# A condition product over 128 rows, a gate-bias product moved, and a new order for an adaLN transformer block

## The chip, the core and the metric

The kernel runs on one NeuronCore of a Trainium2 chip. It is one launch. The metric is the device time of that launch in microseconds; lower is better. The core has five engines with a queue each: TensorE (PE, matmuls and transposes), VectorE (DVE), ScalarE (ACT), GpSimd (POOL) and SyncE (SP, which here issues DMAs). Each engine executes its queue in order and waits on semaphores for the others.

## The reference

A block of a transformer with a condition vector c. Two halves, each behind a layer norm that the condition scales and shifts; the first half is attention over 8 keys at distances 0, 2, ... 14, the second an MLP.

```python
x = A_x                                               # 1 x 2048 x 448, bf16
mod = (silu(c) @ w_mod).reshape(1, 6, 1, 448)         # c is 1 x 448
sa, ca, ga, sb, cb, gb = mod[:, 0], ..., mod[:, 5]
h = layernorm(x) * (1 + ca) + sa
x = x + ga * A_ref(h, A_wqkv, A_wo)                   # 16 heads of 28, window 8, dilation 2
h = layernorm(x) * (1 + cb) + sb
x = x + gb * B_ref(h, B_w1, B_b1, B_w2, B_b2)         # layernorm, 448 -> 1792, tanh-Gelu, 1792 -> 448
```

In B_ref the last step is `h @ w2 + b2`, so the output holds `gb * b2`, the gate-bias product.

## The kernel before

**Tiles.** Even and odd positions are kept apart (`NS = 2`), since the dilation is 2. The 2048 positions are 8 tiles p = 0 to 7 of 2 x 128 positions (`NP = 8`). Attention works on 9 batches of 114 positions of each parity (`NB = 9`), the MLP on 4 pairs of tiles t (`NT = 4`). PSUM is cut into four slots of two banks (room "P"); every PSUM tile lives in one of them.

**A written-out order.** The kernel is a list of tasks (`Plan.add`), each with an engine, a function that issues its instructions, what it reads and writes, and the buffers it uses. `Plan.emit` then issues the tasks in the order of the string `ORDER`; a buffer's slot comes from the list `SLOTS`. So the order of each engine's queue is the order of that engine's tasks in `ORDER`. An entry is a task's number in order of creation; `79:A` puts the task on ScalarE (D: VectorE, P: GpSimd), `88:R` takes TensorE's variant with the half-height rest first, and `52+9@52` first issues 9 filler matmuls of zeros (128x128 by 256 columns, function `filler`, L369) into the PSUM tile of task 52. A task added to the list shifts the numbers of all later ones.

**The head.** `c_cols` (L374) turns the row c into columns: matmuls of c_row, one partition high, with a row of ones, for 4 pieces of 112, each issued twice. From it come `e_c`, `silu`, `silu_bc` (c's silu, broadcast), then `mod_cols` (L390, 40 matmuls: shift and scale of the first norm as columns) and `sca`, which the evacuation of the first transposes needs (`evac_h`, L471: hT = transposed norm x scale + shift). Meanwhile x of tile 0 goes through `stats`, `rstd`, `norm`, `tail` and `tr0` (transposes on TensorE, L506). Tiles 0 to 3 are transposed on TensorE, tiles 4 to 7 by DMA (zT). The q and k weights come from HBM packed (wqk_st for the first 384 rows, wqr_st for the last 64) and are spread to 32 columns a head by `spread` and `spread r` (L412); `qk0_0af0`, ... `qk0_1b` are the q (0) and k (1) products of tile 0 (`f0` to `f2`: the three full contractions; `r`: the half-height rest).

**mods** (L592) computes the other four condition rows (ga, sb, 1 + cb, gb), writes them to HBM (`mod_st`) and loads them back broadcast over the partitions (`mod_bc`, L607). Then VectorE scales wo by ga (`wo_scale`, L610) and w2 by gb (`w2_scale`, L618), and GpSimd makes `gbb2 = gb * b2` (L614). `residual` (L796) adds gbb2 to x for each tile (x1p, GpSimd), and `fin` (L847) adds that to the MLP's output. A one-column copy on GpSimd, `gate` (L826), waits for the first Gelu of an MLP pair, so that the x1p of that pair start no earlier.

**The stages** (loop over `PHASES`): batches 0 to 4 of attention and MLP pair 0; batches 5, 6 and pair 1; batches 7, 8 and pairs 2, 3. Names in what follows: `lt` are the logits of a batch, `pd` its denominators, `po` its outputs (128 matmul and weight-load instructions a batch), `v` its values, `omul` the normalised output, `wo0` to `wo7` the output projections with `x1` (the residual add), `w1_t_g` and `w2_p_n_k` the MLP's products.

Of the kernel before, what the change touches and what calls it, by code (L numbers as in the profile page):

```python
# [9 lines left out]
FP32 = mybir.dt.float32  # L10
BF16 = mybir.dt.bfloat16
# [6 lines left out]
KM, MW = 4, 112  # L18
# [31 lines left out]
]  # L50
ORDER = """
0 13 3 15 1 4 5 14 11 7 16 12 17 8 18 9 10 19 6 52+9@52 2 20 60 21 58 22 61 53 59 54 23 62 55 56 63 57 64 65 24 66
67+13@68 25 68 26 76 70 69 27 77 71 73 72 28 78 74 75 84+10@84 29 85 96 79:A 86 30 82:A 98 31 80:A 97 81 83:A 87+1@90
88:R 32 99 130 100 120 101 90 91 89 92 33 103 93 102 94:R 34 118 104:A 35 121 105 131 119 128 95 36 164 106 129 109:A
179 107:A 37 189 166 108:A 180 122 169 132 190 165 123 187 209 244 38 167 133 188 256 170 110 191 245 168 39 135 210
111:R 171 134 113 40 124 125 112:D 192 114:R 126:A 41 136 127 177 115 137 42 194 150 178 193 139:A 43 138 195 211 44
181 140 151 182 141 212 196 214 172 246 173 215 183 247 147 257 184 174 248 254 185 152 249 45 255 175 258 186 146:R
213 149 251 250 176 259 252:A 143 46 260 253 261 216 262:A 276 145 148:D 153 263 217 277:D 218 219 142 197 200:A 199
198 47 220 48 205:R 49 144 221 50 51 418:A 278 154 281 201 279 155 267 156 207 266 264 159 206:R 282 280 203 160 316
283 265:A 222 162 208 163 527 317 272 161 223 157 284 285 274:D 286 202 287 224 226 269:R 225 288 204 227 158 289 271  # L60
228 318 229 351 290 419 352 230 231 291 273:R 420 293 292 454:A 232 348 294 353 275 313 311 233 295 349 236 296 234
314 268 237 297 298 312 315 299 319 270 346 350 235 300 321 238 301 239 116 320 347 303 354 302 240 322 355 304 117
241 455 305 242:D 356 306 323 243 357 307 528:R 308 456:D 309:A 381 310 324 358 529 563 359 325 326 387 360 328 363
329 327 364 361 382:R 330 389 362 331 365 390 366 391 388 333 368 332 367 397 384 334 383 369 335 385 392:R 370 399
338 400 402 398 336 386 339 404 373 337 371 403 424 374 340 372 395 413 375 393 376 396 401 394 411 417 377 378 341
412 425 343 460 342 379:A 426 421 380 344:A 457 461 414 458 345 462 405 422 415 459 416 406 423 427 428 429 464 407
430 431 564 463 565:D 408 465 506 466 409 490 467 410 491:R 508 507 468 492 493 509 511 494 432 469 495 513 470 496
510 433 512 471 472 434 473 436 501:R 474 435 437 499 475 438 497 439 498 500 477 440 441 476 514 442 502 478 505 443
503 516 479 504 446 526 480 517 444 481 447 445 530 482 566 448 531 533 483 449 515 484 534 532 520 567 451 535 450
568 569 518 485 536 570 521 452 538 519 486 453 571 537 487 539 573 572 522 488:A 540 574 489 575 541 599 576 523 542  # L70
577 524 543 525 600 578 544 545 581 546 579 547 582 615:R 580 548 604 583 603 584 601 605 550 617 586 585 616 549 587
602 551 588 610:R 552 606 591 618 620 609 553 607 555 622 608 554 589 619 556 592 590 557 631 593 611 594 613 612 558
623 614 596 559 560 632 595 561:D 621 562 629 597 598 630 624 633 625 634 626 635 627 628 640:R 636 637 653 656 639
638 657 655 645 644 641 654 643 642 650:R 648 647 646 664 651 652 658 649 665 659 666 667 660 672 661 668 662 673 669
663 674 675 670 671
# [76 lines left out]
def kernel(  # L152
# [65 lines left out]
    c_row = cst.tile([1, D], BF16, name="c_row")  # L218
    one1 = cst.tile([1, 128], BF16, name="one1")
# [21 lines left out]
    one = add("DVE", 0.06, lambda: nc.vector.memset(one1[:], 1.0), writes=["one1"], after=[zero], name="one1")  # L241
# [89 lines left out]
    add("ACT", 0.4, lambda: nc.scalar.dma_start(out=c_row[:], in_=c), writes=["c"], late=1.8, name="load c")  # L331
    tbl0 = add("ACT", 1.28, lambda: nc.scalar.preload_act_table_set(EXP_SET), name="tbl")
    load_x(0, 1)
    KP = (range(KM - 1), range(KM - 1, KM))
# [578 lines left out]
```

## Time and profile before

| | |
|---|---|
| three runs | 175.27, 175.70, 180.20 us; median 175.7 us |
| the profiled execution | 175.99 us, of which the span from the first to the last instruction is 174.3 us |
| TensorE, VectorE, ScalarE, GpSimd busy | 166.9, 117.6, 103.9, 42.0 us |
| instructions on TensorE | 2152 matmuls, 2152 weight loads |
| DMA | 15.12 MB, nearly all of the input in the first 45 us |

The table reads so: TensorE has something in flight for nearly the whole span, and the other engines have room on average, but not in each stage. Durations in the profile's rows overlap where an engine is pipelined; the distance between the starts of two rows is what a group costs in the stream.

### The profile page before, as it was taken

What the parts mean: (1) busy time and instruction counts of PE and PEld (TensorE: products, weight loads), DVE (VectorE), ACT (ScalarE), POOL (GpSimd) and SP (SyncE); (2) the same over time, 40 slices, a digit from 0 to 9 for tenths busy, and PEclk for the clock granted to TensorE, in tenths of its full rate; (3) what the DMA queues carried; (4) which work ended last, traced back from release to release, by engine and by line L of the source; (5) the groups of instructions that cost most, each with busy time, mean ns of one, the idle gap of its engine ahead of it and who ended that gap; (6) DMA issues with size and microseconds to landing.
All of it is one profiled execution on the core that took longest, in us unless ns stands there. A gap on an engine that the chain in (4) does not pass through costs nothing.

```text
span 174.3 us, 4984 instructions
## 1 busy us (share of the span) xinstructions
PE 166.9 (96%) x2152; PEld 85.4 (49%) x2152; DVE 117.6 (67%) x290; ACT 103.9 (60%) x146; POOL 42.0 (24%) x60
## 2 busy tenths in 40 slices
PE   7999989999999999999999999997999999999993
PEld 5876564444434355335564343464444455444562
DVE  6498999869989999897436368966498852200103
ACT  3279688699548994587944926769408730078300
POOL 6000624020020120377000183040007940071000
PEclk9999999999999999999999999999999999999999
DMA  5999979996000033000350100008410018200002
GB/s 162 322 323 314 237 217 249 230 259 203 4 2 4 0 66 60 4 0 0 40 141 4 53 0 0 0 4 86 95 53 2 0 26 113 92 0 0 0 30 79
DMA packets 20708, 15.12 MB, mean 87 GB/s; under 512 B 13705, under 2 KB 19726, under 8 KB 20686
## 3 DMA queue, kind: packets, MB, share of 16 engines
q1 hardware_dynamic: 20684, 14.80, 35.6%
q8 instruction: 17, 0.28, 0.7%
q14 instruction: 5, 0.04, 0.1%
q10 hardware_dynamic: 2, 0.00, 0.0%
HBM read 9.81 MB, written 1.84 MB: 67 GB/s over the span
## 4 chain that ended last, share of the span: by engine, by line
PE 72%; DMA 11%; DVE 10%; issue 2%; SPq 2%; ACT 1%; DVEq 0%
PE p L841 25%; PE p L527 21%; DMA x_all<-in_A_x_dram 8%; PE pw L761 6%; PE p L533 4%; PE pq L527 4%; DMA mod_bc<-mod_hbm 3%; PE pv L527 3%; PE lt L696 2%; PE po L729 2%; PE pv L664 2%; DVE w_s L618 2%; DVE et L709 1%; DVE hT L476 1%; DVE stt L432 1%
## 5 line engine op out<-in xcount | busy, mean ns | idle before, releaser
L822 ACT ACTIVATE hm<-p,b_col 128x512 bf16<-128x512 f32 x56 | 33.9, 690 | 33.4 <-PE p L533 30.8
L841 PE MATMUL p<-w_s,hm 128*128 128x448 bf16 (+1 forms) x238 | 44.4, 342 | 1.6 <-issue 1.6
L527 PE MATMUL p<-yT,w_s 128*128 128x512 bf16 x168 | 38.5, 380 | 0.0
L841 PEld LDWEIGHTS <-hm 128*128 128x128 bf16 x238 | 22.7, 98 | 20.8 <-issue 2.4
L448 POOL TENSOR_TENSOR rs_all<-tv_all,neg_half 128x2 f32<-128x2 f32 x22 | 16.2, 745 | 66.4 <-DVE tv_all L446 50.3
L847 DVE TENSOR_TENSOR x_all<-p,x1p 128x896 bf16<-128x896 f32 (+2 forms) x10 | 9.0, 903 | 25.7 <-PE p L841 25.7
L527 PEld LDWEIGHTS <-w_s 128*128 128x128 bf16 x168 | 15.8, 98 | 21.1 <-issue 3.4
L527 PE MATMUL pq<-hT,Wqk 128*128 128x512 bf16 (+1 forms) x108 | 22.2, 345 | 0.4 <-DVE x_all L768 0.4
L432 DVE BATCH_NORM_STATS2 stt<-x_all 128x6 f32<-128x448 bf16 x32 | 18.7, 609 | 1.2 <-DMA x_all<-in_A_x_dram 1.2
L703 ACT ACTIVATE et<-lt 128x928 bf16<-128x928 f32 x18 | 16.3, 954 | 4.0 <-PE lt L696 4.0
L799 POOL TENSOR_TENSOR x1p<-x_all,gbb_bc 128x448 f32<-128x448 bf16 x16 | 16.2, 1040 | 0.0
L527 PEld LDWEIGHTS <-Wqk 128*128 128x128 bf16 x108 | 9.4, 97 | 10.3 <-issue 3.7
L746 DVE TENSOR_TENSOR qT<-po,den 128x912 bf16<-128x912 f32 x9 | 9.9, 1100 | 6.2 <-ACT den L740 6.2
L709 DVE TENSOR_TENSOR et<-et,mask 128x928 bf16<-128x928 bf16 x18 | 11.3, 633 | 3.6 <-ACT et L703 3.6
L761 PE MATMUL pw<-wo_s,qT 128*128 128x448 bf16 x64 | 13.1, 353 | 0.4 <-DVE qT L746 0.4
L768 DVE TENSOR_TENSOR x_all<-pw,x_all 128x896 bf16<-128x896 f32 x8 | 8.7, 1083 | 6.6 <-PE pw L761 6.6
L738 ACT ACTIVATE den<-pd 128x928 f32<-128x928 f32 x9 | 8.5, 944 | 6.9 <-PE pd L718 6.9
L826 POOL COPY seen<-hm 128x1 bf16<-128x1 bf16 x4 | 3.9, 980 | 31.3 <-ACT hm L822 31.3
L740 ACT ACTIVATE den<-den,den_bias 128x928 f32<-128x928 f32 x9 | 9.6, 1067 | 0.2
L761 PEld LDWEIGHTS <-qT 128*128 128x128 bf16 x64 | 6.1, 98 | 6.5 <-DVE qT L746 0.9
L432 DVE BATCH_NORM_STATS2 stt<-h 128x6 f32<-128x448 bf16 x16 | 9.2, 609 | 0.0
L777 DVE TENSOR_TENSOR h<-h,mod_bc 128x896 bf16<-128x896 bf16 x16 | 9.1, 614 | 0.0
(101 smaller groups left out, 191.1 us busy)
## 6 DMA issues: line engine op xcount, KB each, us to landing
wmod<-in_w_mod_dram SPq DMA_DIRECT2D x4, 392.0 KB, 11.3
w_s<-in_B_w_dram SPq DMA_DIRECT2D x7, 224.0 KB, 4.6
out_dram<-x_all SPq DMA_DIRECT2D x7, 224.0 KB, 2.0
x_all<-in_A_x_dram SPq DMA_DIRECT2D x3, 448.0 KB, 5.4
w_s<-in_B_w_dram SPq DMA_DIRECT2D x3, 448.0 KB, 4.2
wqk_st<-in_A_wqkv_dram SPq DMA_DIRECT2D x3, 225.0 KB
wm_st<-in_w_mod_dram SPq DMA_DIRECT2D x1, 588.0 KB, 4.8
x_all<-in_A_x_dram SPq DMA_DIRECT2D x2, 224.0 KB, 2.6
```

The lines of the kernel that those rows point to most:

```text
L432: add("DVE", 0.53, lambda: nc.vector.bn_stats(out=stt[:, w, b, :], in_=src()), reads=reads, bufs=bufs, after=early if w == b == 0 else (), ...
L448: add("POOL", 0.55 + 0.17 * n, lambda: nc.gpsimd.tensor_tensor(out=r, in0=tv, in1=neg_half[:, 0:n], op=ALU.pow), reads=[f"tv{w}_{b0}", "ne ...
L527: nc.tensor.matmul(out(), lhsT=lhs(kt, slice(0, 128)), rhs=rhs(kt, slice(0, 128)), start=first and kt == 0, stop=not first and kt == KT - 2)
L703: exps.append(add("ACT", 0.83, lambda half=half, lt=lt: nc.scalar.activation(out=et.t[:, 2 * half:2 * half + 2].rearrange("p r m c -> p r ...
L709: nc.vector.tensor_tensor(out=ev, in0=ev, in1=mask[:], op=ALU.mult)
L740: exps.append(add("ACT", 0.96, lambda: nc.scalar.activation(out=den.t[:], in_=den.t[:], func=ACT.Exp, scale=-1.0, bias=den_bias[:]), bufs= ...
L746: nc.vector.tensor_tensor(out=qT[:, :, LEAD + q00:LEAD + q00 + 2 * WQ], in0=po.t[:, :, 0:NS * 4 * WQ].rearrange("p j (m c) -> p m j c", c=WQ),
L761: nc.tensor.matmul(pw.t[:, s, 0:D], lhsT=qT[:, NS * PLACE[ft] + s, LEAD + 128 * p:LEAD + 128 * p + 128], rhs=wo_s[:, ft, :], start=(ft == ...
L777: add("DVE", 0.55, lambda vec=vec, op=op: nc.vector.tensor_tensor(out=h2.t[:], in0=h2.t[:], in1=vec.unsqueeze(1).to_broadcast([128, NS, D] ...
L799: add("POOL", 1.0, lambda n=n: nc.gpsimd.tensor_tensor(out=x1p.t[:, n, :], in0=xn(p, n), in1=gbb2_bc[:], op=ALU.add), reads=[f"x{p}", "gbb ...
L822: gelus.append(add("ACT", 0.585, lambda f=f, a=a, p1=p1s[g]: nc.scalar.activation(out=hm.t[:, f].rearrange("p n c -> p (n c)"), in_=p1.t[: ...
L841: nc.tensor.matmul(p2.t[:, n, 0:c1 - c0], lhsT=hm.t[:, f, n, q * 128:(q + 1) * 128], rhs=w2_s[:, f, c0:c1], start=(f == parts[0][0]), stop ...
```

## The change

Four edits. **c_row** becomes 128 partitions high; VectorE fills it with zeros first (new task `c0`, number 1), the DMA writes c into its first row, `one1` is 128 rows of ones, and `c_cols` contracts over 128 rows, once for each of the 4 pieces instead of twice. **gbb2** is created in `mlp` for pair 0, behind `gate`, instead of in `mods`. The **zero matmuls** go from 33 (9 before c_cols, 13 before mod_cols, 10 and 1 in qk0) to 25 (11, 10, 4). **ORDER and SLOTS** are new lists.

```diff
-    c_row = cst.tile([1, D], BF16, name="c_row")
-    one1 = cst.tile([1, 128], BF16, name="one1")
+    c_row = cst.tile([128, D], BF16, name="c_row")
+    one1 = cst.tile([128, 128], BF16, name="one1")
...
-    one = add("DVE", 0.06, lambda: nc.vector.memset(one1[:], 1.0), writes=["one1"], after=[zero], name="one1")
+    zero_c = add("DVE", 0.17, lambda: nc.vector.memset(c_row[:].bitcast(FP32), 0.0), writes=["c"], after=[zero], name="c0")
+    one = add("DVE", 0.1, lambda: nc.vector.memset(one1[:], 1.0), writes=["one1"], after=[zero_c], name="one1")
...
-    add("ACT", 0.4, lambda: nc.scalar.dma_start(out=c_row[:], in_=c), writes=["c"], late=1.8, name="load c")
+    add("ACT", 0.4, lambda: nc.scalar.dma_start(out=c_row[0:1, :], in_=c), writes=["c"], late=1.8, name="load c")
...
-        for k in [*range(KM)] * 2:
-            nc.tensor.matmul(psc.t[0:MW, 0, 128 * k:128 * k + 128], lhsT=c_row[0:1, k * MW:(k + 1) * MW], rhs=one1[:], start=True, stop=True)
-
-    add("PE", 0.9, c_cols, mode="32x128", reads=["c", "one1", "warm_w"], bufs=[psc], fills=[psc], name="c_cols")
+        for k in range(KM):
+            nc.tensor.matmul(psc.t[0:MW, 0, 128 * k:128 * k + 128], lhsT=c_row[:, k * MW:(k + 1) * MW], rhs=one1[:], start=True, stop=True)
+
+    add("PE", 0.45, c_cols, mode="F", instr=8, reads=["c", "one1", "warm_w"], bufs=[psc], fills=[psc], name="c_cols")
...
-        add("POOL", 1.05, lambda: nc.gpsimd.tensor_tensor(out=gbb2_bc[:], in0=gb_bc, in1=b2_bc[:], op=ALU.mult),
-            reads=["gb", "b2"], writes=["gbb2"], port=True, name="gbb2")
...
+        if t == 0:
+            add("POOL", 1.05, lambda: nc.gpsimd.tensor_tensor(out=gbb2_bc[:], in0=gb_bc, in1=b2_bc[:], op=ALU.mult),
+                reads=["gb", "b2"], writes=["gbb2"], port=True, after=[gate], name="gbb2")
```

The two lists, read out by the tasks' names, where the queues differ most (`#` counts the tasks of one name in order of creation; in `stats` and `norm`, #5 and #6 belong to tile 2, #7 and #8 to tile 3, #9 to #12 to tiles 4 and 5, #17 and #18 to tile 6, #19 and #20 to tile 7):

```
ScalarE, head
 before: load c, table load, e_c, ln, rstd, silu_bc, evac_h#1, evac_h#3, spread r x4, ln#2, rstd#2, evac_qk#1, ...
 after:  table load, load c, ln, e_c, rstd, silu_bc, spread#4, evac_h#1, spread r#2, evac_h#3, spread r#1, ln#2, ...
VectorE, from tile 2's stats on
 before: ... evac_h#5, aggr#7, stats#10, stats#12, aggr#10, tv#1, tv#2, aggr#12, stats#11, stats#17, aggr#11, stats#20,
         tv#4, aggr#17, mask#1, norm#8, mask#2, norm#7, norm#5, norm#6, ...
 after:  ... stats#10, aggr#5, evac_h#8, tv#1, stats#19, stats#17, aggr#19, stats#12, aggr#17, aggr#10, stats#20,
         norm#8, norm#7, aggr#20, norm#5, stats#11, mask#2, aggr#11, tv#8, norm#6, ...
SP, behind the w1 loads
 before: zT5, mod_st, w2l0, zT4, w2l1, zT6, mod_bc, zT7, w2l2, w2l3, w2l4, w2l5, w2l6
 after:  w2l0, w2l1, mod_st, w2l2, w2l3, zT4, zT5, zT7, mod_bc, zT6, w2l4, w2l5, w2l6
TensorE, qk0
 before: qk0_0af0, 0af1, 0af2, (1 zero), 0ar, 0b, 1af0, 1af1, 1af2, 1ar, 1b
 after:  qk0_0af0, 0af1, 1af0, 1af1, 0af2, 0ar, 0b, 1af2, 1ar, 1b
TensorE, from mods to wo0
 before: lt1 x2, pd0, po0, qk2_1b, qk2_1a, qk2_0b, v2, pd1, po1, qk2_0a, qk4_1a, lt2 x2, qk4_0a, qk4_1b, lt3_1, wo0
 after:  lt1 x2, b1, qk2_0b, qk2_0a, qk2_1a, pd1, qk2_1b, pd0, po1, v3, lt2 x2, v2, po0, qk4_1b, v5, po2, pd2, wo0
TensorE, batches 7 and 8
 before: ..., lt8_1, pd7, w2_3_0_1, po7, po8, pd8, w2_3_1_0, wo6, w2_3_1_1, wo7, w1_2_0, ...
 after:  ..., lt8_1, w2_2_0_1, w2_3_0_0, po7, pd7, w2_3_1_0, w2_3_1_1, po8, pd8, w2_3_0_1, wo6, w1_2_0, w1_2_6, wo7, ...
```

Twenty-eight other tasks change their engine, mostly evacuations that either ScalarE or VectorE can do. `spread#4`, the k half of the weight spread (128x1536), goes from VectorE to ScalarE.

More of the change, by code (lines that the diff above doesn't have):

```diff
@@ L57 @@
[L57 to L61, printed above, removed]
@@ new lines @@
+101 87 131 88 102 89:R 34 103 132 104 35 93 130 121 94 90 36 95:R 133 105:D 122 134 119 37 106 96 179 164 120 110 38
+107:A 123 254 124 109:A 244 169 108:A 166 255 189 39 165 209 245 180 256 167 136 40 135 170 114 257 125 187 137 210
+115:R 171 41 188 177 111 116 258 126 190 259 178 112:R 42 246 127:A 181 191 43 247 182 128 248 113 138 44 261 151
+142:A 45 139 249 141 211 46 152 192 140 214 47 212 117 144 153 251 215 193 213 48 183 216 143:R 184 49 194 185:D 250
+168 147 252:A 118 195 146:D 186 217 260 148 149:D 219 196 262:A 145:D 220 172 218 150 311 263 221 174 278 175 312:D
@@ L76 @@
+646:R 637 640 654 658 639 638 657 656 665 647 648 655 650 673 649 669 674 661 675 676 662 659 660 666 663 670 667 664
+671 668 672
 """
```

36 lines of the change are left out of this document (17 added, 19 removed), and 10 rows, old and new, of the table SLOTS.

## The prediction

> **What bounds the kernel now.** I read the page first: busy times, then the chain that ended last.
>
> ```profile
> span 174.3 us, 4984 instructions
> ...
> PE 166.9 (96%) x2152; PEld 85.4 (49%) x2152; DVE 117.6 (67%) x290; ACT 103.9 (60%) x146; POOL 42.0 (24%) x60
> ...
> PE 72%; DMA 11%; DVE 10%; issue 2%; SPq 2%; ACT 1%; DVEq 0%
> ```
>
> TensorE is busy 96% of the span, and 72% of the chain is TensorE. So an edit is worth what it takes out of TensorE's stream, or out of the waits in that stream. Next I listed those waits, in the timeline of TensorE.
>
> ```profile
> 22.06 1.06 PE L509 MATMUL ptr<-ident,zy 128*128 128x128 bf16 x16
> ...
> 24.18 0.37 PE L598 MATMUL pb<-wmod,silu_bc 112*32 112x448 bf16 x4 [0.31 <-DMA wmod<-in_w_mod_dram]
> ...
> 25.30 0.44 PE L696 MATMUL lt<-qT,kT 28*64 28x58 bf16 x32 [0.38 <-DVE hT L476]
> ...
> 26.55 1.47 PE L527 MATMUL pq<-hT,Wqk 128*128 128x512 bf16 x6
> ...
> 31.50 1.64 PE L664 MATMUL pv<-Wv,hT 128*64 128x448 bf16 x16
> ...
> 46.23 1.45 PE L527 MATMUL pq<-hT,Wqk 128*128 128x512 bf16 x6 [0.42 <-DVE x_all L768]
> ...
> 50.03 1.69 PE L761 MATMUL pw<-wo_s,qT 128*128 128x448 bf16 x8 [0.41 <-DVE qT L746]
> ```
>
> ```profile
> 122.43 1.49 PE L841 MATMUL p<-w_s,hm 128*128 128x448 bf16 x7 [1.57 <-issue]
> ```
>
> Five waits, 0.31 + 0.38 + 0.42 + 0.41 + 1.57 = 3.09 us, are nearly all there is after the first 14 us. The last and largest is ended by "issue": TensorE waited for no engine and no tile. The changed kernel issues the same matmuls after that point, and counting from the two orders, its stream changes array shape as often (83 times in both), so nothing is won or lost there. What can change is the head, and these waits.
>
> **The head: c_cols, the zeros, the queues.** The old head:
>
> ```profile
> 0.80 0.50 ACTq L331 DMA_DIRECT2D c_row<-in_c_dram  x1
> ...
> 1.33 1.28 ACT L332 ACT_TABLE_LOAD   x1 [1.33 <-PEq L897]
> ...
> 1.59 0.81 DVE L301 MEMSET wo_s<- 128x896 f32 x1 [0.23 <-issue]
> ...
> 3.16 1.10 PE L377 MATMUL ps_c<-one,c_row 1*112 1x128 bf16 x8
> 3.39 1.16 DVE L432 BATCH_NORM_STATS2 stt<-x_all 128x6 f32<-128x448 bf16 x2 [0.32 <-DMA x_all<-in_A_x_dram]
> ...
> 6.93 1.06 PE L509 MATMUL ptr<-ident,zy 128*128 128x128 bf16 x8
> ...
> 7.31 0.29 DVE L419 COPY Wqk<-wqk_st 128x512 bf16<-128x512 bf16 x1 [1.01 <-DMA wqk_st<-in_A_wqkv_dram]
> ...
> 9.43 1.02 ACT L478 ACTIVATE hT<-ptr,mod_col 128x256 bf16<-128x256 bf16 x2 [3.80 <-DVE mod_col L409]
> ...
> 10.34 1.43 ACT L428 COPY Wqr<-wqr_st 64x256 bf16<-64x256 bf16 x4
> ...
> 11.52 0.39 PE L533 MATMUL pq<-hT,Wqr 64*128 64x256 bf16 x3 [0.17 <-ACT Wqr L428]
> ...
> 12.71 1.01 ACT L587 CAST qT<-pq 128x1024 bf16<-128x1024 f32 x1
> ```
>
> ```profile
> L369 PE MATMUL ps_col<-warm_w x13: 393/421/421, 4.2 to 6.7; 128*128 128x256 bf16 x13
> L369 PE MATMUL pq<-warm_w x11: 272/273/283, 9.1 to 10.9; 128*128 128x256 bf16 x11
> ```
>
> The zero-fill of c_row is a new VectorE memset of 224 fp32 per partition; by wo_s (896 in 0.81) it is about 0.2 us, and VectorE has 0.32 idle before the first x arrives: nothing. The c load now waits for it and stands behind the table load: issued at about 2.1 instead of 0.8. Eleven zero matmuls at the old spacing (nine from 1.12 to about 3.04, 0.213 each) end at 3.5, so c is about in time, and four full-height matmuls replace eight one-row ones (about 0.55 less). The old head has TensorE at half speed until some time between 6.7 and 9.1 (421 ns, then 273 ns for the same matmul). If full-height c_cols let it speed up earlier, the first transposes (8 in 1.06 at 6.93) shrink by about half a microsecond.
>
> But the new ScalarE queue puts the k half of the weight spread (`spread#4`, 128x1536) ahead of the first hT evacuation. It needs all three wqk loads: the first is in at 7.3, the other two at about 8.5 (an estimate: 450 KB at 0.37 MB per us, the mean of this window).
>
> ```profile
> 7.30:8.00 0.70, 0.70 (x14) 0.70 (x12) 0.29 (x1) 0.00 (x0) 0.00 (x0) 1.00 1.06 385
> 8.00:8.60 0.60, 0.60 (x30) 0.56 (x26) 0.00 (x0) 0.00 (x0) 0.00 (x0) 1.00 1.10 351
> ```
>
> ScalarE takes 0.36 for 256 columns and 1.01 for 1024, so about 1.45 for 1536: until 10.0. Then hT (0.51), one Wqr copy (0.36), hT (0.51), one Wqr copy (0.36): Wqr is complete at about 11.75, where the old one let TensorE go at 11.52. From there the old stream took 2.73 us to the end of qk0 at 14.25; the new one has two k pieces (0.44) behind it already: 14.05. The head gives at most 0.2, and the next paragraph takes that away.
>
> **x for tiles 6 and 7.** In the chain and in VectorE's timeline:
>
> ```profile
> 9.47 8.77 DMA x_all<-in_A_x_dram
> ```
>
> ```profile
> 15.99 1.15 DVE L432 BATCH_NORM_STATS2 stt<-x_all 128x6 f32<-128x448 bf16 x2 [0.53 <-DMA x_all<-in_A_x_dram]
> ...
> 18.26 0.63 DVE L432 BATCH_NORM_STATS2 stt<-x_all 128x6 f32<-128x448 bf16 x1 [0.32 <-DMA x_all<-in_A_x_dram]
> ...
> 19.55 0.61 DVE L709 TENSOR_TENSOR et<-et,mask 128x928 bf16<-128x928 bf16 x1
> ...
> 20.93 1.00 DVE L452 TENSOR_SCALAR zy<-x_all,mvs,rs_all 128x448 bf16<-128x448 bf16 x3
> ```
>
> The loads' order on SP is unchanged, so x[6:8] still lands at 18.24. The old VectorE came to its first use at 17.9; the new queue has it (`stats#19`) earlier, right after one hT evacuation and `tv#1`. After x[4:6] at 15.97 stand one stats (0.53), an aggr, an hT and tv, so VectorE is there at about 17.0 and waits 1.2. Behind it stand the norms of tiles 2 and 3, for which TensorE's tr2 waits: five stats at 0.53, four norms at 0.31, one mask at 0.54, small ones 0.5: 4.9 us, done at 23.2 against 21.9. TensorE wants tr2 at 22.06: a new wait of 1.1. The waits of 0.31 and 0.38 behind it (w_mod in at 24.15; hT) are then covered by it, but hT of tiles 2 and 3 comes about 0.9 later too. I take +0.6 net; from -0.3 (x earlier, old waits gone) to +1.4.
>
> **gbb2.** GpSimd's product now waits for the first Gelu:
>
> ```profile
> 38.08 2.00 DVE L610 TENSOR_TENSOR wo_s<-wo_s,mod_bc 128x896 bf16<-128x896 bf16 x2 [0.81 <-DMA mod_bc<-mod_hbm]
> ...
> 40.98 0.61 DVE L618 TENSOR_TENSOR w_s<-w_s,mod_bc 128x896 bf16<-128x896 bf16 x1
> ```
>
> ```profile
> 38.14 1.46 POOL L614 TENSOR_TENSOR gbb_bc<-mod_bc,b_bc 128x448 f32<-128x448 bf16 x1 [8.95 <-DMA mod_bc<-mod_hbm]
> ```
>
> Beside it the two wo_scale took 2.00, where two of that shape take at most 1.22 (the w2_scale of 0.61): 0.78 goes away, just where VectorE feeds TensorE's waits of 0.42 and 0.41. I take these two in full, -0.83, bounds 0 and -0.83. Behind the first gate the product delays four x1p and two rstd by 1.5; their users, the final adds and the norms of tiles 2 and 3, wait for TensorE in between, so I put nothing on it. Nor on the end, where the same stores leave in another order.
>
> **The wait at 120.9.** Just before it TensorE ran its two densest groups back to back, and one instruction packet was in flight:
>
> ```profile
> 118.97 1.36 PE L729 MATMUL po<-et,vb 64*32 64x57 bf16 x128
> ```
>
> ```profile
> q8 instruction: 17, 0.28, 0.7%
> ```
>
> ```profile
> q8 instruction: 1, 0.02, 5.7%
> ```
>
> Seventeen packets carry 4304 TensorE instructions, so 256 each; the one in the stretch 119.2 to 121.3 took 5.7% of 16 engines over 2.1 us, that is 1.9 us of one. The two po are 256 instructions in 1.3 us: TensorE used up a whole packet while the next was on its way. The new order puts pd7 and two w2 parts (2.9 us) between po7 and po8: -1.57, bounds 0 and -1.57. Its densest place is now lt2, v2, po0 (288 instructions in 2.9 us): less dense, but among weight loads. I take +0.3, from 0 to +1.57.
>
> **Sum.** 0 (head) + 0.6 - 0.83 - 1.57 + 0.3, and 0.2 for waits of the new order that I don't see (bounds 0 and 1.5, the old order's first four): -1.3. The profiled execution took 175.99 us (span 174.3); 174.7, which is 1.0 under the median of 175.7.
>
> **Rivals.** (1) Everything fits: x[6:8] is in by 17, no new wait, all five old ones go, and the head's 0.85 (0.45 of cold transposes, 0.4 of later start) reaches the end: 175.99 - 3.09 - 0.85 = 172.05. For it: the head does shed half-speed work. Against: VectorE's order above. [...]
>
> (2) Slower: mod_bc comes late. Its issue now stands behind four w2 loads and the transposes of tiles 4, 5 and 7.
>
> ```profile
> 32.96 0.61 SPq L607 DMA_DIRECT2D mod_bc<-mod_hbm  x1
> 33.66 2.02 SPq L501 DMA_TRANSPOSE zT<-zy  x1
> ```
>
> ```profile
> 32.96 5.04 DMA mod_bc<-mod_hbm
> ```
>
> Tile 7's last norm stands 5.3 us of VectorE work behind hT of tiles 2 and 3 (26.5 in my reading): 31.8, two transposes later 34.5, plus 5.04: 39.5, and with two wo_scale and a w2_scale between them 41.1. TensorE reaches wo0 after five q/k groups (1.65 each, 26.55 to 31.50), three v (1.64), three po and pd and two lt, some 16.5 us after 26.5: 43.0. From a landing at 41.3 on, each microsecond is TensorE's. At 44 it costs 2.7: 177.4; at 46 over 179.
>
> (3) The change doesn't do what it says: with 1.4 us of idle before qk0 and fewer zeros, half speed lasts until about 15. That doubles some 2 us of qk0, of which the wait for tr2 hides 1.1: +0.9, 175.6.
>
> **Chances.** Forecast 0.45, (1) 0.27, (2) 0.18, (3) 0.10. About 2% (172.2 to 179.2) is what a measurement of this kernel can tell from no change. Faster than that: most of (1) and the low edge of the forecast, 0.24. Slower: the far part of (2) and waits that I don't see, 0.14. Same: 0.62. The range goes from 171.4 (under (1)) to 179.2 (well into (2)); the forecast's own is 173.2 to 176.4.
>
> **What would show it.** Right: VectorE's stats on tile 7 waiting for x near 18.2 with over 0.8 idle; tr2 near 23; wo_scale twice about 0.6; no "issue" wait near 120; ScalarE's 128x1536 copy until about 10. Wrong: tr2 on time, a wait for wo0 on VectorE near 43, zero matmuls or qk0 at 421 ns after 9 us, or a new "issue" wait of over 1 us.

## The result, and the profile after

The changed kernel took 177.61 us (median of 4, 177.42 to 177.74) beside 175.49 for the kernel before: a ratio of 1.0131, 95% interval 1.0100 to 1.0162. The ratios here and below leave out executions over 1.5% above their kernel's fastest: one of 180.20 among these four of the kernel before, two of four in e3, eight of twelve in e5. The forecast was 174.7, so the time moved the other way. The profiled execution took 177.69 us with a span of 175.7; before, 175.99 and 174.3. A later series on another chip (e5 below) had twelve executions of the same changed kernel from 173.06 to 180.06: this spread is part of the result.

The page of the kernel after, same parts as before:

```profile
span 175.7 us, 4964 instructions
...
PE 166.8 (95%) x2140; PEld 83.9 (48%) x2140; DVE 119.5 (68%) x292; ACT 104.4 (59%) x142; POOL 41.0 (23%) x63
...
PEclk9965999999999999999999999999999999999999
...
PE 89%; DMA 3%; issue 2%; ACT 1%; SPq 1%; DVE 1%; ACTq 0%; DVEq 0%
```

TensorE is as busy as before (166.8 of 166.9). The row that differs is PEclk: each digit is a slice of 4.39 us, and the third and fourth slices (8.8 to 17.6 us) were granted six and five tenths of full speed. Before, the mean granted clock of the execution was 1.000; here 0.981. TensorE's head shows it (start, duration, then what ended the idle time ahead):

```profile
6.27 0.85 PE L510 MATMUL ptr<-ident,zy 128*128 128x128 bf16 x8
6.96 1.32 PE L398 MATMUL ps_col<-silu_bc,wm_st 112*128 112x32 bf16 x40
8.62 0.60 PE L370 MATMUL pq<-warm_w 128*128 128x256 bf16 x4 [0.35 <-DVE mod_col L410]
11.10 2.29 PE L550 MATMUL pq<-hT,Wqk 128*128 128x256 bf16 x10 [1.88 <-ACT hT L479]
...
17.27 0.61 PE L510 MATMUL ptr<-ident,zy 128*128 128x128 bf16 x8
```

TensorE idles 1.88 us ahead of qk0, and then qk0 takes 6.17 us (11.10 to 17.27) where it took 4.03 (10.22 to 14.25): 3.02 us late at its end. Of the 3.02 us, 0.88 is the later start and 2.14 the longer run. ScalarE's timeline says whom it waited for:

```profile
0.80 1.28 ACT L333 ACT_TABLE_LOAD   x1 [0.80 <-PEq L899]
1.34 0.49 ACTq L332 DMA_DIRECT2D c_row<-in_c_dram  x1
...
9.12 1.47 ACT L422 COPY Wqk<-wqk_st 128x1536 bf16<-128x1536 bf16 x1 [2.51 <-DMA wqk_st<-in_A_wqkv_dram]
10.49 0.56 ACT L479 ACTIVATE hT<-ptr,mod_col 128x256 bf16<-128x256 bf16 x1
```

The 128x1536 copy is `spread#4`; it waits for the last wqk load and holds the first hT until 10.49. The view by stretches (stretch, length, busy times, then the granted clock as the third column from the end) cut where the clock changed:

```profile
3.38:6.79 3.41, 3.41 (x22) 2.32 (x21) 2.54 (x10) 0.83 (x4) 0.29 (x1) 1.00 1.03 297
6.80:10.20 3.40, 2.07 (x49) 1.76 (x48) 1.84 (x8) 1.08 (x1) 0.00 (x0) 1.00 1.07 301
10.21:13.62 3.41, 2.52 (x14) 1.41 (x13) 3.33 (x11) 2.50 (x7) 0.00 (x0) 0.50 1.07 332
13.63:17.03 3.40, 3.40 (x20) 1.72 (x17) 2.12 (x9) 1.01 (x1) 0.70 (x1) 0.50 1.09 322
17.04:20.45 3.41, 3.41 (x98) 2.22 (x97) 2.53 (x9) 2.98 (x5) 0.69 (x1) 1.00 1.02 249
```

The clock was up from 6.80, went to half at 10.21, and came back at 17.04: steps of 3.41 us. (1.00 in the first row is only the view's figure ahead of the first change on record; the zeros there still start 0.213 us apart, and 0.11 from 8.62 on.) Behind the head, the waits of TensorE in sum, and the place of the largest:

```profile
PE po L728 <- issue: 2.3, 1, 2.3
PE pq L550 <- ACT hT L479: 1.9, 1, 1.9
PE ps_c L370 <- DVE warm_w L240: 1.1, 1, 1.1
PE pq L370 <- DVE mod_col L410: 0.4, 1, 0.4
```

```profile
39.47 0.62 PE L728 MATMUL po<-et,vb 64*32 64x57 bf16 x57
42.39 0.22 PE L728 MATMUL po<-et,vb 64*32 64x57 bf16 x7 [2.30 <-issue]
```

All five waits of before are gone, the one at 120.9 included. One new one stands inside po0: from one matmul's start to the next 2.47 us more than its columns need.

In these traces the place of such a stop goes with how many instructions came before, and not with what stands there. Counted from 0 in each trace, the matmul that starts after such a stop is number 1885 in the kernel before, e4, e7, e8, e13 and e14, and number 607 in the changed kernel, e1, e5, e10 and e11. The 1278 matmuls between, each with its weight load, are 2556 instructions, ten packets of 256 less four. I call such a place the boundary, and the place 256 instructions ahead of it the crossing. At both places, in all 16 traces, the next packet starts between 0.1 us ahead of the crossing and 2.7 us behind it. (Elsewhere in the stream the packets' starts fit such a count less well; no stop stands there.) Here the crossing was passed at 37.33, the packet ran from 40.01 to 40.93, and the boundary was reached at 39.90; before, 119.01, 119.27 to 121.19, and 120.51. In both, TensorE was at the boundary ahead of the packet's end, and waited. At the other of the two places it came to the boundary some 3 us behind the packet's end (here 126.16 and 123.19, before 37.72 and 34.56), and did not stop.

So the account is: +3.0 at the end of qk0, -1.6 in the waits behind it (by the distance between starts, about 4.1 that went, 2.7 that came, and small change), together +1.4 in the span, and +0.3 outside the span: 1.7, from 175.99 to 177.69.

### The profile page after: what moved, and what is told of

Read it like the earlier page. It is cut to its first block, busy times and chain, and to the rows that moved or that the text cites. A ratio compares the mean times of both kernels' runs of the same rounds, so it can differ in the third digit from the quotient of the medians.

```text
span 175.7 us, 4964 instructions
## 1 busy us (share of the span) xinstructions
PE 166.8 (95%) x2140; PEld 83.9 (48%) x2140; DVE 119.5 (68%) x292; ACT 104.4 (59%) x142; POOL 41.0 (23%) x63
## 4 chain that ended last, share of the span: by engine, by line
PE 89%; DMA 3%; issue 2%; ACT 1%; SPq 1%; DVE 1%; ACTq 0%; DVEq 0%
PE p L843 24%; PE p L528 21%; PE pq L528 12%; PE pw L760 7%; PE pv L663 4%; PE p L534 4%; DMA wqk_st<-in_A_wqkv_dram 3%; PE po L728 3%; PE lt L695 3%; PE pq L534 3%; PE pv L528 3%; PE pq L550 2%; PE pd L717 1%; DVE x_all L849 1%; ACT Wqk L422 1%
## 5 line engine op out<-in xcount | busy, mean ns | idle before, releaser
L528 PE MATMUL pq<-hT,Wqk 128*128 128x512 bf16 (+1 forms) x108 | 23.2, 357 | 0.0
L798 POOL TENSOR_TENSOR x1p<-x_all,gbb_bc 128x448 f32<-128x448 bf16 x16 | 17.4, 1116 | 0.1
L528 PEld LDWEIGHTS <-Wqk 128*128 128x128 bf16 x108 | 9.9, 101 | 10.7 <-issue 3.5
L776 DVE TENSOR_TENSOR h<-h,mod_bc 128x896 bf16<-128x896 bf16 x16 | 12.4, 804 | 0.1
L588 ACT CAST kT<-pq 128x1024 bf16<-128x1024 f32 x7 | 7.1, 1014 | 4.2 <-PE pq L528 2.1
L588 ACT CAST qT<-pq 128x1024 bf16<-128x1024 f32 x5 | 5.1, 1011 | 7.4 <-PE pq L534 4.3
L453 DVE TENSOR_SCALAR h<-x_all,mvs,rs_all 128x448 bf16<-128x448 bf16 x16 | 7.3, 487 | 3.0 <-POOL rs_all L449 3.0
```

The lines of the kernel that those rows point to most:

```text
L528: nc.tensor.matmul(out(), lhsT=lhs(kt, slice(0, 128)), rhs=rhs(kt, slice(0, 128)), start=first and kt == 0, stop=not first and kt == KT - 2)
L588: add("ACT", 0.13 + m * n / 1310, lambda dst=dst, src=src: nc.scalar.copy(out=dst, in_=src()), bufs=[pqs[i]], writes=w, alt={"DVE": (0.07 ...
L776: add("DVE", 0.55, lambda vec=vec, op=op: nc.vector.tensor_tensor(out=h2.t[:], in0=h2.t[:], in1=vec.unsqueeze(1).to_broadcast([128, NS, D] ...
L798: add("POOL", 1.0, lambda n=n: nc.gpsimd.tensor_tensor(out=x1p.t[:, n, :], in0=xn(p, n), in1=gbb2_bc[:], op=ALU.add), reads=[f"x{p}", "gbb ...
```

## Experiments

Each was timed beside the kernel before on the same chip. "Mean clock" is an execution's mean granted TensorE clock; one step of 3.413 us at half speed makes 0.99 of it, two make 0.98.

| run | median us (n) | before | ratio, 95% interval |
|---|---|---|---|
| e1 spread#4 on VectorE | 174.22 (10) | 175.96 | 0.9892, 0.9853 to 0.9930 |
| e2 22 zeros | 175.64 (10) | 175.96 | 0.9961, 0.9924 to 0.9998 |
| e3 po0 later | 175.10 (4) | 175.96 | 0.9879, 0.9817 to 0.9942 |
| e4 before, c_cols edit alone | 175.91 (10) | 175.96 | 1.0012, 0.9964 to 1.0060 |
| e5 the changed kernel again | 176.67 (12) | 176.03 | 0.9880, 0.9825 to 0.9935 |
| e6 three mends | 175.21 (12) | 176.03 | 0.9961, 0.9929 to 0.9994 |
| e7 before, gbb2 alone | 175.51 (10) | 176.03 | 0.9957, 0.9918 to 0.9996 |
| e8 before, small zeros | 175.11 (10) | 176.03 | 0.9943, 0.9904 to 0.9983 |
| e9 22 zeros of 32 rows | 176.25 (12) | 176.27 | 0.9997, 0.9960 to 1.0033 |
| e10 head reordered | 176.66 (12) | 176.27 | 0.9996, 0.9954 to 1.0039 |
| e11 one transpose late | 177.58 (10) | 176.27 | 1.0076, 1.0036 to 1.0115 |
| e12 before, 4 zeros | 174.02 (4) | 176.27 | 0.9893, 0.9848 to 0.9937 |
| e13 before, 4 zeros and gbb2 | 173.98 (6) | 176.44 | 0.9858, 0.9816 to 0.9899 |
| e14 as e12, same count | 176.23 (12) | 176.44 | 0.9993, 0.9958 to 1.0029 |

For e3, e5 and e11, whose spread is the effect under study, the medians and mean clocks say more than the ratio.

**The clock in the head: e1, e2.**

```diff
-... 79 82:A 29 76 30 74 99 ...
+... 79 29 76 30 74 82 99 ...
```

> The changed kernel with one task put elsewhere: the k half of the weight spread (spread#4, 128x1536) stands on VectorE behind its second hT evacuation, and no longer on ScalarE ahead of its first. Theory A (the clock): the loss is TensorE's 1.9 us of idle ahead of qk0, in which the granted clock fell to half from 10.2 to 17.0; without the wait qk0 begins by about 10.0, the clock stays up, qk0 ends near 14 and not at 17.3, and the time falls by about 2.9, to 174.7. Theory B (instruction packets): the loss is the 2.47 us of 'issue' inside po0; the head costs little in the end, since later waits take it up; the time stays within 0.5 of 177.6. Theory C (the head waits for the weights, not for ScalarE's order): qk0 begins as late as before this edit, the clock falls as before, 177.6.

Seven of the ten executions had a mean clock of 0.998 or more, three 0.99; none 0.98. The profiled one:

```profile
9.14 0.69 PE L550 MATMUL pq<-hT,Wqk 128*128 128x256 bf16 x4 [0.27 <-ACT hT L479]
10.06 0.61 PE L550 MATMUL pq<-hT,Wqk 128*128 128x256 bf16 x4 [0.23 <-DVE Wqk L420]
11.28 0.38 PE L550 MATMUL pq<-hT,Wqk 128*128 128x256 bf16 x2 [0.61 <-ACT hT L479]
...
13.89 0.65 PE L510 MATMUL ptr<-ident,zy 128*128 128x128 bf16 x8
```

qk0 begins at 9.14 and ends at 13.89. Theory A holds for the clock and the time (174.2), and C falls: the order on ScalarE set the start. The wait in po0 shrank too, to 0.2, with no instruction moved in TensorE's order; that surprised me and led to e11. The head ends 3.4 us earlier and po0 waits 2.1 less, yet the time is only 3.4 under 177.6: waits behind them, 0.9 for yT the largest, take up the rest.

```diff
-81:A 85+4@85 75
+81:A 85+22@85 75
```

> The changed kernel with 22 zero matmuls in place of 4 ahead of qk0; ScalarE's order as it is, so qk0 can't begin before about 11.1. Theory A: TensorE is never idle from 8.6 to 11.1, the clock stays up, each 512-column matmul of qk0 takes 0.22 us and not 0.43, qk0 ends at about 14.3, and the time falls by about 2.9, to 174.7. Theory D (the clock falls for another reason, such as the total work of the first 10 us): it falls at 10.2 just the same, 177.6 or a little more. The 36 instructions more also move every boundary between instruction packets; the wait of 2.47 inside po0 may change by that, up to 2 us either way.

```profile
8.67 2.56 PE L370 MATMUL pq<-warm_w 128*128 128x256 bf16 x22 [0.86 <-DVE mod_col L410]
11.08 1.38 PE L550 MATMUL pq<-hT,Wqk 128*128 128x256 bf16 x10
```

qk0 starts as late as in the changed kernel (11.08), but its ten matmuls take 1.38 and not 2.29. No execution of ten was under 0.997. Theory D falls. The median is 175.6 and not 174.7: in the profiled execution TensorE waited 0.5 for the norms that tr2 needs and 0.8 for yT, two waits that the changed kernel, later there, does not show.

**Not every time: e3, e5.**

```diff
-200 173 280 282 206 50
+200 280 282 206 173 50
```

> The changed kernel with po0 (128 instructions in 0.65 us) moved behind the next group of q/k matmuls (16 instructions in 1.6 us) in TensorE's order. Theory B: TensorE used up a packet of 256 instructions (lt2, v2, most of po0) in 2.6 us while the next packet was late; with 1.6 us more the wait of 2.47 falls to under 1 us; the head is unchanged; 177.6 - 1.6 = 176.0. Rival E: the packet only starts when the DMA transposes and the mod_bc rows in flight are through (it started at 40.0, when they ended), so the wait falls by just the 1.6 us that are put ahead of it, but what TensorE does meanwhile is useful work, so the time falls by the same; the two differ where the packet starts: by B near 38.3, one microsecond behind the crossing at 37.3 as elsewhere, by E at 40.0 again. Theory A says nothing of it, its 3 us in the head stay.

The wait in po0 was gone, but the packet started at 34.45, 0.16 behind its crossing at 34.29, so the run does not tell B from E. What it showed was not asked: this kernel's head is the changed kernel's, and yet two executions (173.50, 173.59) had a clock of 1.000, two (176.61, 177.85) 0.977 and 0.981. The profiled one idled 1.65 ahead of qk0 and kept its clock:

```profile
5.03:8.44 3.41, 2.80 (x57) 2.37 (x56) 2.09 (x11) 0.71 (x5) 0.00 (x0) 1.00 1.06 338
8.45:11.85 3.40, 1.75 (x17) 1.08 (x14) 3.21 (x11) 3.33 (x7) 0.00 (x0) 1.00 1.09 324
```

qk0 ended at 13.98. The grid of 3.413 us stood elsewhere: its step edge at 8.44 let the zeros' end, the idle time and qk0's first matmuls share one step, where the changed kernel's edge at 10.21 cut them apart.

The changed kernel again, no edit:

> The changed kernel unaltered, timed more often beside the others, for its spread. In the profiled executions so far the granted clock changes only on a grid of 3.413 us, and the grid stood at another place in each of them (first full speed at 8.35, 6.80, 6.82, 5.84, 5.03, 4.89); the variant with po0 moved has the same head as this kernel and its executions went two ways, mean clock 1.000 (173.5) and 0.98 (176.6, 177.9). Theory A2: the head's 1.9 us of idle is only counted against TensorE where enough of it falls within one step of the grid, and that is chance from one execution to the next: of the executions some have a mean clock of 0.98 and about 177.6, others 1.00 and 174.5 to 175.2. Theory A1 (the idle closes the clock every time in this kernel): all at 0.98 and 177.4 to 177.8.

Of twelve executions two had a mean clock of 1.00 (173.06, 173.74), five 0.99 (173.77 to 177.41), five 0.981 or less (176.33 to 180.06). Theory A2 holds. With the first four, 14 of 16 lost at least one step; the mean clock does not say where, and in e11 below it is po0's stop that cost the step. Nor is the clock all of the spread: the five at 0.99 differ by 3.6 us. Of the kernel before, 12 of the 106 executions timed beside these runs were at 0.99. The two with the clock up beat every execution of the kernel before (174.97 at best on that chip): there the change is a gain.

**Work in the array or time busy: e9.** In each trace I summed, per step of the grid, the columns that TensorE streamed times the share of its array that each matmul used (rows times columns over 16384, the 128*128 of the largest). I count 8192 as a full step, an estimate: at half speed the zeros, 256 columns each, start every 0.213 us, which makes 4096 in 3.413 us, and at full speed every 0.11 us, which makes twice that. In the changed kernel's step from 6.80: 40 mod_cols of 32 columns at 112 rows are 1120, 4 zeros of 256 are 1024, the end of the transposes 110: 2254 of 8192 possible, and the next step ran at half speed. In e3 the step from 8.44 has 3200, and the clock stayed.

```diff
+        r = 32 if n == 22 else 128
-            ... lhsT=warm_w[:, 0:128], rhs=warm_w[:, 0:256], start=True, stop=True)
+            ... lhsT=warm_w[0:r, 0:128], rhs=warm_w[0:r, 0:256], start=True, stop=True)
...
-85+4@85
+85+22@85
```

> The changed kernel with 22 zero matmuls ahead of qk0, as in the earlier run with 22, but these 22 contract over 32 rows and not 128: TensorE is busy just as long, on a quarter of its array. Counted over the ten traces so far, columns times the share of the array that they use, per step of 3.413 us: every step with 2955 or less was followed by half speed, every step with 3168 or more by full speed, whatever the idle time (a step with 1.65 us idle stayed up, one with 1.30 did not). Theory J (the clock follows the work done in the array): 22 small zeros are worth 5.5, so the clock falls in the head about as often as in the changed kernel (10 of 12 executions at 0.99 or under), median 176 to 177.5. Theory K (it follows the time TensorE is busy): as with 22 full zeros, no execution under 0.995, median near 175.6.

```profile
5.95:9.35 3.40, 2.98 (x60) 2.53 (x59) 2.18 (x11) 1.04 (x2) 0.00 (x0) 1.00 1.07 323
9.36:12.77 3.41, 3.41 (x18) 2.12 (x16) 3.06 (x10) 2.85 (x7) 0.00 (x0) 0.50 1.08 331
12.78:16.18 3.40, 3.40 (x19) 1.92 (x17) 2.43 (x10) 0.00 (x0) 0.71 (x1) 0.50 1.07 332
```

The step 9.36 to 12.77 is busy from end to end (3.41 of 3.41), yet the next runs at half speed still: its work is 1575. Ten of eleven executions were at 0.99 or less (a twelfth took 907 us and is not used), as in the changed kernel; with 128 rows, none of ten. Theory J holds, K falls. Over all 16 traces, of 19 steps with a work of 2955 or less, 18 were followed by half speed (the other, 2881 in e10, stayed up); of some 760 with 3040 or more, none. The steps ahead of the first change on record are counted as half speed, by the zeros' 0.213 us.

**The parts one by one: e4, e12, e7.** The kernel before with the change's c_row, one1, load c and c_cols lines, and the zero-fill ahead of load c:

> The kernel before with the first edit alone: c_row of 128 zero-filled rows, four full-height matmuls in c_cols in place of eight one-row ones; zeros, order and gbb2 as before. Theory A: the edit itself does no harm: the clock opens near 6.8 and not at 8.35, the first transposes and mod_cols run at full speed, and with ten zeros ahead of qk0 TensorE is idle under 0.7 us, so the clock stays up; 175.5 or up to 0.5 under it. Rival F: the edit is what makes the clock fall: it opens one window earlier, and the next window (6.8 to 10.2) then holds the idle time ahead of qk0 whatever the number of zeros; the clock falls at 10.2, qk0 takes 2 to 3 us longer, 177.5 to 178.5.

The clock was up from 4.89, one of ten executions was at 0.99, as often as in the kernel before, and the time is the same: theory A holds in the time, F falls. The wider contraction by itself neither wins nor loses more than the 0.6% of the interval.

```diff
-84+10@84 ... 87+1@90
+84+4@84 ... 87
```

> The kernel before with 4 zeros ahead of qk0 in place of 10, and without the single one inside: the change's 'fewer zeros' alone. Theory A and J: the old head has ScalarE's hT at once, so qk0 begins at 10.2 as before, the steps lose 6 x 256 of work of some 5300 to 6000 and stay over 3168, so the clock does not fall in the head: 175.5 to 176.2, as the kernel before. Theory L (the zeros are the loss, whatever ScalarE does): the clock falls, mean clock 0.99 or under in most executions, 177.5.

```profile
10.20 0.83 PE L549 MATMUL pq<-hT,Wqk 128*128 128x256 bf16 x6 [0.32 <-ACT hT L478]
```

All four executions at 1.00: theory L falls. Fewer zeros alone did not close the clock; ScalarE's hT is early here (0.32 of idle ahead of qk0). But the time was 1.07% less, which no theory had: the wait at 120 was gone (e14).

gbb2 alone, by the lines of the change's diff:

> The kernel before with the gbb2 edit alone: GpSimd's product behind the first gate, everything else as it was. By the prediction's term: the two wo_scale on VectorE take 1.2 together and not 2.00, and TensorE's waits of 0.42 and 0.41 right behind them shrink: 0 to -0.83, so 174.7 to 175.5. Rival H: those two waits hang on other work (the rstd and mod_bc) and stay: same time; the product then stands beside the w2 or x1 work behind the first Gelu and costs nothing there, since the final adds wait for TensorE. Rival I: beside it h2 norms on VectorE take 0.80 and not 0.61 (as in the changed kernel), up to +0.4.

```profile
38.69 1.15 DVE L610 TENSOR_TENSOR wo_s<-wo_s,mod_bc 128x896 bf16<-128x896 bf16 x2
```

1.15 for the two and not 2.00, and TensorE's waits of 0.42 and 0.41 are not in its list any more. But this execution was the longest of the ten, and TensorE came to that place over 1 us later than before, behind a wait of 0.97 for an hT, so the list alone proves little. The pair e12 and e13 below, one without and one with this edit, is cleaner; these two lines are in e12's list and not in e13's:

```profile
PE pq L527 <- DVE x_all L768: 0.6, 1, 0.6
...
PE pw L761 <- DVE qT L746: 0.4, 1, 0.4
```

In e7's time, 0.43% is 0.75 us, nearly the whole of the term; the interval allows 0.1 to 1.4.

**The wait between instruction packets: e8, e11, e14.** Thirteen zeros of 256 columns become 26 of 128:

```diff
+        c = 128 if n == 13 else 256
-        for _ in range(n):
+        for _ in range(2 * n if n == 13 else n):
-            ... t.sums[0].t[:, 0, 0:256], lhsT=warm_w[:, 0:128], rhs=warm_w[:, 0:256]
+            ... t.sums[0].t[:, 0, 0:c], lhsT=warm_w[:, 0:128], rhs=warm_w[:, 0:c]
```

> The kernel before with 26 zero matmuls of 128 columns in place of 13 of 256 ahead of the first mod_cols: as much work for TensorE, 26 instructions more, so every boundary between packets of 256 instructions comes 26 instructions earlier. Theory B: the wait of 1.57 to 1.74 at 120.5 hangs on where the boundary stands: the packet that started at 119.27, beside the DMA transposes of 119.0 to 121, now starts at about 118.3, ahead of them, and is in by 119.5, so the wait falls under 0.5 and the time by about 1.3, to 174.3. Rival E2: the wait hangs on the transposes, whatever the boundary: it stays over 1 us; 175.6.

```profile
118.04 1.20 PE L729 MATMUL po<-et,vb 64*32 64x57 bf16 x124
120.28 0.21 PE L729 MATMUL po<-et,vb 64*32 64x57 bf16 x4 [1.04 <-issue]
```

The wait moved into the end of po8, 26 instructions earlier, and fell only to 1.04: a miss for B, which had under 0.5, and E2's bound is met but not its reason, since the wait moved with the boundary. The packet ran from 117.39 to 118.78, earlier than before, but TensorE reached the boundary earlier too (119.05) and went on only 1.5 us after the packet was in.

```diff
-154 276 253 279 ... 51 419:A 52 283
+154 276 279 ... 51 419:A 52 253 283
```

> The changed kernel with one DMA transpose (tile 6) issued behind the last three w2 loads and not ahead of them. Its first use lies some 12 us later, so nothing waits for it. Rival E (an instruction packet waits behind the DMA transposes in flight): in the traces of the changed kernel the packet after the crossing at 35.9 and 37.3 started 2.3 and 2.7 us after it, when the transposes were through, and TensorE waited 1.9 and 2.5 in po0; with the spread moved, the crossing at 34.2 came ahead of the transpose, the packet started 0.7 after it, and the wait was 0.36. With the transpose out of the way the packet starts within 1.3 us of the crossing and the wait in po0 is under 1.0, wherever the head puts it; the time falls by 1 to 1.5. Theory B (only how fast TensorE uses up the packet counts): the wait stays at 1.9 or more.

```profile
36.23 0.62 PE L728 MATMUL po<-et,vb 64*32 64x57 bf16 x57
38.95 0.22 PE L728 MATMUL po<-et,vb 64*32 64x57 bf16 x7 [2.10 <-issue]
```

E falls as I had put it: the wait is 2.10 with that transpose out of the way. The packet still started late, at 36.35, 2.3 behind the crossing at 34.09, now beside the rows of mod_bc and the w2 loads. In e1, with the crossing at 34.22 and transposes moving, it started 0.7 behind. The nine traces of the changed kernel and its variants point at mod_bc, which moves as 128 packets of 3584 bytes: in the three where the instruction packet started 2.3 to 2.7 us late (the changed kernel, e5, e11), 109 to 116 of the 128 started between the crossing and its start; in the other six, where it started 0.1 to 1.2 behind, none did. No run moves mod_bc alone, so this is a lead and not shown.

This trace also has a loss of clock that is not the head's. In its head TensorE idled 1.66 ahead of qk0 and kept full speed; the step with po0's stop, busy for 1.31 of 3.41 us, was followed by half speed:

```profile
36.50:39.91 3.41, 1.31 (x46) 0.75 (x36) 0.94 (x2) 2.46 (x3) 0.00 (x0) 1.00 1.19 227
39.92:43.32 3.40, 3.40 (x11) 0.87 (x10) 3.40 (x8) 1.66 (x3) 0.00 (x0) 0.50 0.20 44
```

The kernel of e12, with its 14 missing instructions put back as smaller zeros ahead of mod_cols (6 of 256 columns, 14 of 128):

```diff
-        for _ in range(n):
+        for i in range(20 if n == 13 else n):
+            c = 128 if n == 13 and i >= 6 else 256
```

> The kernel before with 4 zeros ahead of qk0, and 14 instructions put back ahead of mod_cols (13 zeros of 256 columns become 6 of 256 and 14 of 128: as much work), so that from the end of qk0 on every instruction has the number it has in the kernel before, and the boundary at 120 falls on the same matmul. Theory B (the boundary's place makes the wait): the 'issue' wait of 0.8 to 1.7 near 120 is back, and the time is 1.0 to 1.7 above that with 4 zeros alone: 0.995 to 1.0 of the kernel before. Theory E (the transfers in flight make it): the wait is as in the run with 4 zeros alone, under 0.3, and the ratio 0.989.

First e12 without them, then e14:

```profile
118.42 1.35 PE L729 MATMUL po<-et,vb 64*32 64x57 bf16 x128
119.58 0.42 PE L718 MATMUL pd<-et,ones_k 64*32 64x464 bf16 x8
119.93 1.69 PE L841 MATMUL p<-w_s,hm 128*128 128x448 bf16 x8
```

```profile
119.94 0.36 PE L841 MATMUL p<-w_s,hm 128*128 128x448 bf16 x1
121.71 1.49 PE L841 MATMUL p<-w_s,hm 128*128 128x448 bf16 x7 [1.41 <-issue]
```

Same order, same transfers (the two transposes issued from 118.10 and 118.09 on), same time of arrival at 119.9: fourteen instructions, and the wait is 1.41 or nothing. The packet was in at 119.78 in e12 and at 120.45 in e14; TensorE went on 1.2 to 1.5 us after that in four traces with such a stop (listed at the end), so by my estimate even the earlier packet would have held it for 1.0 at e14's boundary, reached at 119.95. Theory B holds: the place of the boundary made this wait. 0.9893 became 0.9993.

**Put together: e6, e10, e13.** Spread on VectorE, ScalarE's second hT ahead of the Wqr copies, 6 and 4 zeros, po0 later:

```diff
-79 82:A 29 76 30 74 99 31 73 83 32 100 97 81:A 85+4@85 75 84 86 33 98 91 ... 200 173 280 282 206
+79 29 76 30 74 82 99 31 73 83 32 100 97 75 81:A 85+6@85 84 86 33 98 91+4@91 ... 200 280 282 206 173
```

> The changed kernel with the k half of the spread on VectorE behind its second hT, ScalarE's second hT ahead of the Wqr copies that wait for wr, 6 zeros ahead of qk0 and 4 ahead of its k part, and po0 behind the next q/k group. Theory A: qk0 ends near 13.3 (13.9 with the spread moved alone, where ScalarE's second hT stood behind a wait for wr), no idle stretch over 0.5 us in the head, mean clock 0.995 or more in every execution; by theory B no instruction wait over 0.5 us near 37. Together 172.5 to 173.5 in most executions, beating both kernels. Rival G: what the head wins is lost again at the waits behind it (b1_rows landed at 24.9 with the spread moved, the norms of tiles 2 and 3), so that no more than 174.2 comes of it.

175.2, so rival G by the time: the clock held in eleven of twelve executions, and the gain was lost behind the head. Where, no trace shows for these eleven: the profiled execution is the twelfth, at 177.28 the longest, and lost a step of its head to half speed (10.41 to 13.82). It waited 0.9 for yT and 0.7 for an hT at the place that po0 had left.

```diff
-71 78 28 70 72 79 82:A 29 76 30 74 99 31 73 83 32 100 97 81:A 85+4@85 75 84 86 33 98 91 ... 542 ... 601 ... 578
+71 70 72 78 28 79 29 76 30 74 82 99 31 73 83 32 100 97 75 81:A 85+8@85 84 86 33 98 91+4@91 ... 542 ... 578 601
```

> The changed kernel with the head put in another order and one part of the end: the k half of the spread on VectorE behind its second hT; VectorE's two mod_col sums ahead of the second spread that waits for wqk; ScalarE's second hT ahead of the Wqr copies that wait for wr; 8 zeros ahead of qk0 and 4 ahead of its k part; po0 where the change has it; wo7 ahead of the first group of the third first-layer stage, where TensorE waited 0.8 to 1.1 for the transposes. Theory A and J: the steps of the head hold over 3168 of work, so no execution under 0.985 and few under 0.995; qk0 ends near 13.5; the wait near 123 goes: 172.5 to 173.8, under both kernels. Rival G: what the head wins is lost at the next waits: 174.2, as with the spread moved alone.

A miss: the clock held in all twelve (0.997 to 1.000), qk0 ended at 13.9, and the gain was lost behind it. The profiled execution, at 178.08 the longest of the twelve, shows these waits among others:

```profile
PE pw L760 <- DVE x_all L767: 1.7, 1, 1.7
...
PE po L728 <- issue: 0.8, 1, 0.8
PE pv L663 <- ACT hT L479: 0.6, 1, 0.6
```

wo7 in its new place waits for x_all, longer than the wait that it was to cover.

The kernel before with 4 zeros and the gbb2 edit:

> The kernel before with two edits of the change, and its old order otherwise: 4 zeros ahead of qk0 (none inside), and gbb2 behind the first gate. By the two alone (0.989 with four executions, 0.996): 0.985, so 173.2 where the kernel before takes 175.8. Rival M: the 0.989 was luck of four executions and the wait at 120 comes and goes by itself; then 0.995, 175.

0.9858: the two add up as far as the intervals (0.4% each way) can tell, and M falls. By the median this is the fastest of the versions tried, 173.98, under both kernels; e12 and e1 are within its interval. One instruction wait of 0.41 is left, at 121.2.

## Why the prediction was wrong, point by point

- **The head, term 0.** This is the step that failed. "Wqr is complete at about 11.75 ... 14.05" took TensorE's full speed for granted through the idle time ahead of qk0, and so the term was 0. ScalarE was busy until 10.59 (I said 10.0; the last wqk load was in at 9.1 and not at 8.5), which costs some 0.6; where the clock stayed up qk0 ended at 13.98 (e3) and 14.68 (e2). In the profiled execution the clock fell to half at 10.21 and qk0 ended at 17.27: +3.0.
- **Rival (3)** came nearest: idle ahead of qk0 and fewer zeros, half speed. Its size and its chance were off. I had half speed last from the start until 15, 2 us doubled, 1.1 of it hidden by the wait for tr2: +0.9, chance 0.10. In the trace the clock was up from 6.80, fell at 10.21 and came back at 17.04; TensorE did not wait for tr2, so that hid nothing. Fourteen of 16 executions lost a step or more somewhere. Where the steps lie differs from trace to trace (full speed from 8.35 before, 6.80 in the changed kernel, 4.43 in e5, 5.03 in e3). Idle time alone does not tell which step is followed by half speed: the changed kernel's from 6.80 was, with 1.3 us of idle, e3's from 8.44 was not, with 1.65, and e9's from 9.36 was, with none.
- **Rival (1)** had a gain from earlier full speed through the new c_cols. In e4, with that edit alone, the clock was up from 4.89 and before from 8.35, but where the steps lie differs from trace to trace, and the time is the same: no run shows the gain.
- **x for tiles 6 and 7, +0.6.** It did not come in the changed kernel's trace. VectorE waited 0.2 for x in all:

```profile
L433 DVE BATCH_NORM_STATS2 stt<-x_all 128x6 f32<-128x448 bf16 x32 | 18.6, 609 | 0.4 <-DMA x_all<-in_A_x_dram 0.2
```

  What failed here is "x[6:8] still lands at 18.24": the load was in by 16.4, and VectorE, behind the late head, came to it at 18.31. The landing differs from execution to execution, 15.2 (e11) to 18.2 (before) over the 16 traces. Where it is late and the head is on time, the term comes as forecast: in e2 x was in at 17.9, VectorE, ready at 17.1, waited 0.88 for it, and TensorE waited 0.50 at tr2. e10 has the same pair, 0.86 and 0.49. In e1 and e3, with x in by 15.4 and 15.3, tr2 does not wait.

```profile
17.97 1.15 DVE L433 BATCH_NORM_STATS2 stt<-x_all 128x6 f32<-128x448 bf16 x2 [0.88 <-DMA x_all<-in_A_x_dram]
```

```profile
23.45 1.06 PE L510 MATMUL ptr<-ident,zy 128*128 128x128 bf16 x15 [0.50 <-DVE zy L453]
```

- **gbb2, -0.83.** Right in what goes away, and in size as far as it was measured: the two wo_scale take 0.62 each, the two waits are gone in e13 beside e12, and e7's time is 0.75 us less (0.1 to 1.4). Behind the first gate the product takes 1.08 and TensorE waits for nothing there.
- **The wait at 120.9, -1.57.** It went. With po7 and po8 apart, the 256 instructions from crossing to boundary take 5.3 us (120.84 to 126.16) where they took 1.5 (119.01 to 120.51), and the packet was in at 123.19. But e14 shows that the dense pair is only half of the cause; the boundary's place is the other: without those 14 instructions, in e12, the wait was gone with the pair as it was.
- **The new densest place, +0.3.** The place was right (lt2, v2, po0), the size was not: 2.30 of idle, beyond my bound of 1.57. I bounded it by the old wait, where the packet started 0.3 us after the crossing; here it started 2.7 after (37.33 to 40.01). Why so late stays open; the count under e11 points at mod_bc's rows.
- **mod_bc, rival (2).** wo0 ran at 46.54 without a wait for it; not it. **c_cols**: c was issued at 1.34, inside the table load, not at 2.1 behind it; c_cols ran at 3.50 as said.

In sum: -1.3 forecast against +1.7. The head's 3.0 and the packet's 2.2 beyond its +0.3 are 5.2; the absent wait of 0.6 and the old waits, which went nearly all, give back 2.5 of it, and 0.3 is outside the span. The four executions timed first, 177.42 to 177.74, do not show the spread of e5's twelve; that all four had lost two steps was chance.

## What to carry to other kernels

Before moving work ahead of TensorE's first large matmuls, add up what TensorE's array does in every 3.4 us of the head, in whatever phase: where a stretch can fall to the work that was followed by half speed here (2955 or less of 8192), price half speed for the step that follows. Full-height matmuls in that stretch kept the clock here (e2, none of ten executions under 0.997), as many of 32 rows did not (e9, ten of eleven at 0.99 or less). Time such a head over a dozen executions: the first four here all fell on one side. The "issue" wait beside dense short matmuls hung on the instruction count here (1.41 us or none, by 14 instructions): try a few instructions more or less ahead of such a wait before rebuilding an order.

## What the hardware showed that I had not expected

- In these traces the granted clock went with the work in the array and not with the time busy: steps at 2955 or less of 8192 were followed by half speed (18 of 19), steps at 3040 or more by full speed (all of some 760). e9 varies the rows alone; that the columns count in the same way is my reading. So it was in mid-kernel too: in e7 a step from 119.06 with the two po and a wait of 1.4 (work 1963) was followed by 3.4 us at half speed, and in e11 the one with po0's stop.
- After the late packet was in, TensorE went on 1.2 to 1.5 us later: 121.19 to 122.43 before, 40.93 to 42.39 after, 118.78 to 120.28 in e8, 120.45 to 121.71 in e14.
- With the 128-row c_row, about 0.3 us more of the execution lies outside the span: 1.8 to 2.5 in its ten traces (1.97 in e4's), 1.7 to 1.8 in the six without it. What it is, no run tells.
